# Sliding attention and a GeGLU block on one core: ones of the crossed units in their own tile, clears and spreads of both pairs in one GpSimd instruction, another order of the staged v, and other PSUM banks for one unit's scores

## The chip, the core and the metric

The kernel runs on one core of a Trainium2 chip. The metric is the device time of one execution in microseconds, as the median of several runs. Names used below: PE is TensorE, DVE is VectorE, ACT is ScalarE, POOL is GpSimd and SP is SyncE, which only issues DMAs here. A "q" behind an engine's name means its sequencer, which waits and issues.

## The reference

The inputs are q, k and v of 8 batches, 8 heads, 576 tokens and 64 dimensions each, and three weight matrices. Heads 0 to 3 attend to the last 32 tokens ("plain"), heads 4 to 7 to every fourth of the last 128 ("dilated"). The heads' outputs, put side by side, are the 4608 x 512 input of a gated feed-forward block.

```python
scores = scale * np.matmul(q, k.transpose(0, 1, 3, 2))
rel = pos[:, None] - pos[None, :]
mask_plain = (rel >= 0) & (rel < 32)
mask_dil = (rel >= 0) & (rel < 128) & (rel % 4 == 0)
attn = softmax(np.where(masks, scores, -1e9))       # heads 0-3 plain, 4-7 dilated
x = np.matmul(attn, v)                              # to 4608 x 512
g, val = x @ w_gate, x @ w_val                      # 512 -> 1536
out = (0.5 * g * (1 + erf(g / sqrt(2))) * val) @ w_out
```

## The kernel before

**Units.** The attention of one batch is cut into four units of two heads each; the two heads of a unit lie on the two halves of the 128 partitions. Unit n belongs to batch n // 4. In batches 0, 1 and from 4 on, the first two units of a batch are plain and the last two dilated; in batches 2 and 3 it is the other way round (`pair`, `is_plain`). A batch's two plain units share tiles for q, k and v, and so do its two dilated ones; the index g (0 or 1) says which of the two units is meant and x which half of the partitions.

**Steps of a unit.** A program in words gives the order in which each engine gets its work. `S4@2` is the scores of unit 4 in PSUM bank 2 and the one after it, `P4` the exp on ACT, `M4` the multiplication with a mask on DVE, `D4` the sums (a matmul with ones), `T4` and `B4` or `A4` the reciprocal of the sums, `N4` the matmul with v, `X4` the product of both into `xT`. `t8` to `t15` are the transposes of q and k of batch 1 by matmul (`turn_first`). A digit alone is so many matmuls of the feed-forward block. `g` and `u` are the gelu on ACT and the product on DVE that makes `u_all`; `e0` to `e3` are the copies of 128 output rows to one of four `osb` buffers, each followed by a store that SP issues. `E` and `G` load ACT's tables. `V`, `V1`, `F2` and `H2` are `second()`, `second_v()`, `load_first(2)` and `load_rest(2)`, which issue loads and the work of POOL for the coming batches.

**Block-diagonal tiles.** For batches from 1 on, the scores and `N` are matmuls over all 128 partitions. A block of k or v is 128 x 128 with the two heads in two of its four 64 x 64 quarters and zeros in the others. In the second unit (g = 1) the heads stand crossed: the head of half x goes to column half 1 - x. `zero()` clears the unused quarters, with one memset per g and x; `spread()` copies k into the used quarters from `dense`; `cast_v()` does this for v out of `stage`. The sums of crossed units need crossed ones, so `two_ones` has two 128 x 128 parts: part 0 is set by DVE at the start, part 1 by two POOL memsets in `second()`.

**Feed-forward.** The 4608 rows go through in nine chunks of 512. A chunk has 96 matmuls for gate and value (L635) and 48 for the output (L642). The units of a batch stand between those of the chunk that comes before its rows. In chunk 0 the last gate (block 11) is in bank 2 and its value in bank 3.

**Queues around the change.** POOL runs in the order written: `second()` comes after batch 0's units and issues, behind its clears, the loads of batch 1's q and k (`six`, then `load_eights`, both with a cast to f16), the last weights and `wo` in three pieces. SP runs in its order too: the v loads of batch 1 (`load_v(1, ...)`) wait for the second `wo` piece to land, then come `load_first(2)`, two stores, `load_rest(2)` with four DMA transposes (L267) and eight small and large loads of dilated v (L244, L248), a store, `load_first(3)` and then the store of `e3` of chunk 0 with those of chunk 1.

**Lines that the prediction uses.** L107 and L116 are POOL's first instructions (`identity`, `bands`), L132 the end of the masks, L152 and L155 the weight loads, L175 `load_eights`, L200 the memset in `zero`, L215 and L227 the casts of q and k, L256 the cast in `cast_v`, L275 the copy in `spread`, L323 the tail of dilated q, L364 and L360 the copies in `turn_first` on DVE and ACT, L382 its transposes, L441 the matmuls of units, L503 the exp, L653 the copies `e`, L657 the stores, L728 the memsets of `two_ones` in `second()`, L804 the product `u`.

## Time and profile before

| | |
|---|---|
| median of 6 runs | 342.13 us (341.26 to 343.46) |
| the profiled execution's own time | 341.77 us |
| its span (first to last instruction) | 340.1 us |
| granted clock of PE | 1.00 |
| PE busy | 327.3 us |
| DVE, ACT, POOL busy | 157.5, 157.7, 153.9 us |
| moved by DMA | 47.96 MB, mean 141 GB/s |

The profile is one execution. Its first part gives busy times of the engines, its fourth the chain of work that ended last. Beside the page the trace can be asked who waited for whom, for a timeline of an engine in a stretch of time (start, length, engine, line, operation, tiles, shapes, count, and in brackets the idle time before and what ended it), and for the busy shares in given stretches. Times in timelines count from the start of the span. A line of a timeline can hold several instructions of a kind; its length then reaches over all of them.

### The profile page before, as it was taken

How to read it: one execution, taken by the hardware profiler on the slowest of the kernel's cores; microseconds unless marked ns; L12 is line 12 of the kernel's file. 1: busy time of each engine (PE TensorE's matmuls, PEld its weight loads, DVE VectorE, ACT ScalarE, POOL GpSimd, SP SyncE). 2: the span in 40 equal slices, each digit the busy share in tenths (PEclk: the TensorE clock that was granted, in tenths of full speed). 3: DMA queues.
4: the chain of work that ended last, by engine and by line, in shares of the span. 5: the costliest groups of instructions: out<-in, count | busy, mean ns of one | idle time of the engine just before them, and what ended most of it. 6: DMA issues, size and time to landing. Idle time of an engine off the chain costs nothing.

```text
span 340.1 us, 7089 instructions
## 1 busy us (share of the span) xinstructions
PE 327.3 (96%) x2780; PEld 164.0 (48%) x2780; DVE 157.5 (46%) x245; ACT 157.7 (46%) x235; POOL 153.9 (45%) x291
## 2 busy tenths in 40 slices
PE   7899899998979999999999999999999999999995
PEld 5654454443534455445554454445544444444443
DVE  6764454443624445432585365367854424303310
ACT  2663466534653358436943573345534343223321
POOL 8799877759335746835944762682000000000000
PEclk9999999999999999999999999999999999999999
DMA  8999995897689589769889947982100110020002
GB/s 188 185 181 151 201 187 139 207 213 173 153 275 201 139 224 197 201 168 215 154 230 214 188 152 180 249 149 83 64 0 3 63 62 2 0 93 33 0 31 95
DMA packets 109250, 47.96 MB, mean 141 GB/s; under 512 B 83872, under 2 KB 104736, under 8 KB 109216
## 3 DMA queue, kind: packets, MB, share of 16 engines
q1 hardware_dynamic: 97440, 39.99, 50.8%
q0 software_dynamic: 11216, 6.79, 14.1%
q10 hardware_dynamic: 560, 0.72, 0.8%
q8 instruction: 22, 0.36, 0.4%
q14 instruction: 12, 0.10, 0.1%
HBM read 37.75 MB, written 9.44 MB: 139 GB/s over the span
## 4 chain that ended last, share of the span: by engine, by line
PE 76%; DMA 9%; POOL 7%; SPq 4%; issue 1%; ACT 1%; DVE 1%; POOLq 0%; DVEq 0%; ACTq 0%
PE ps L635 44%; PE ps L642 24%; PE ps L441 4%; PE ps L452 3%; DMA xT<-in_q_dram 2%; DMA xT<-in_k_dram 2%; DMA out_dram<-osb 2%; SPq L208 1%; DMA dense<-s 1%; DMA stage<-in_k_dram 1%; POOL wv L152 1%; POOL wg L152 1%; POOL v L256 1%; POOL q L200 1%; PE ps L666 1%
## 5 line engine op out<-in xcount | busy, mean ns | idle before, releaser
L804 DVE SCALAR_TENSOR_TENSOR u_all<-g,ps 128x512 f16<-128x512 f16 x108 | 73.8, 687 | 111.7 <-PE ps L635 100.3
L635 PE MATMUL ps<-xT,wv 128*128 128x512 f16 x432 | 112.8, 379 | 2.2 <-ACT osb L653 2.2
L635 PE MATMUL ps<-xT,wg 128*128 128x512 f16 x432 | 114.2, 379 | 0.4 <-ACT g L799 0.2
L799 ACT ACTIVATE g<-ps 128x512 f16<-128x512 f32 x108 | 64.0, 597 | 108.2 <-PE ps L635 108.0
L642 PE MATMUL ps<-wo,u_all 128*128 128x512 f16 x420 | 99.0, 379 | 0.0
L635 PEld LDWEIGHTS <-wv 128*128 128x128 f16 x432 | 42.2, 98 | 50.6 <-issue 0.3
L635 PEld LDWEIGHTS <-wg 128*128 128x128 f16 x432 | 41.6, 98 | 51.8 <-issue 3.7
L642 PEld LDWEIGHTS <-u_all 128*128 128x128 f16 x420 | 38.0, 98 | 39.9
L275 POOL COPY q<-dense 64x512 f16<-64x512 f16 (+1 forms) x84 | 40.5, 519 | 20.3 <-DMA dense<-s 12.5
L256 POOL CAST v<-stage 64x576 f16<-64x576 f32 x60 | 41.0, 684 | 7.3 <-DMA stage<-in_v_dram 4.4
L503 ACT ACTIVATE P<-ps 128x832 f16<-128x832 f32 (+1 forms) x32 | 26.7, 834 | 21.3 <-PE ps L441 15.6
L626 DVE TENSOR_TENSOR xT<-ps,rb 128x576 f16<-128x576 f32 x32 | 29.8, 935 | 14.5 <-PE ps L452 9.8
L653 ACT ACTIVATE osb<-ps 128x512 f32<-128x512 f32 x34 | 20.2, 593 | 28.8 <-PE ps L642 23.6
L215 POOL CAST s<-stage 128x640 f16<-128x640 f32 x24 | 16.6, 718 | 33.6 <-DMA stage<-in_q_dram 21.3
L227 POOL CAST s<-stage 128x512 f16<-128x512 f32 x24 | 14.4, 631 | 11.2 <-DMA stage<-in_q_dram 6.7
L508 DVE TENSOR_TENSOR P<-P,two_d 128x768 f16<-128x768 f16 x14 | 9.1, 649 | 16.4 <-ACT P L503 16.4
L441 PE MATMUL ps<-q 128*128 128x96 f16 (+2 forms) x225 | 13.4, 203 | 1.7 <-POOL q L323 0.9
L605 ACT ACTIVATE lg<-ps 128x576 f32<-128x576 f32 x17 | 11.1, 650 | 7.5 <-PE ps L452 6.5
L441 PEld LDWEIGHTS <-q 128*128 128x128 f16 x225 | 11.3, 98 | 5.8 <-issue 1.9
L508 DVE TENSOR_TENSOR P<-P,two_p 128x832 f16<-128x832 f16 x14 | 8.6, 616 | 10.6 <-ACT P L503 9.0
L452 PEld LDWEIGHTS <-v 64*64 64x64 f16 x400 | 9.2, 107 | 8.6 <-issue 7.3
L596 DVE STREAM_TRANSPOSE dt<-ps 128x576 f32<-128x576 f32 x15 | 11.6, 775 | 2.5 <-ACT rb L607 1.7
(76 smaller groups left out, 197.9 us busy)
## 6 DMA issues: line engine op xcount, KB each, us to landing
out_dram<-osb SPq DMA_DIRECT2D x35, 256.0 KB, 2.3
stage<-in_v_dram SPq DMA_DIRECT2D x32, 144.0 KB, 3.8
stage<-in_v_dram SPq DMA_DIRECT2D x28, 128.0 KB, 2.7
stage<-in_q_dram SPq DMA_DIRECT2D x24, 128.0 KB, 3.0
stage<-in_k_dram SPq DMA_DIRECT2D x24, 128.0 KB, 2.8
stage<-in_q_dram SPq DMA_DIRECT2D x6, 512.0 KB, 4.4
stage<-in_k_dram SPq DMA_DIRECT2D x6, 512.0 KB, 5.5
wg<-in_moe_w_gate_dram POOLq DMA_DIRECT2D x6, 256.0 KB, 6.6
```

Source lines behind the costliest of these rows:

```text
L256: nc.gpsimd.tensor_copy(dst[half, at, half_of(x, g * swap)], st[half, at])
L275: eng.tensor_copy(dst[half, :, :, half_of(x, g)], src[half])
L441: nc.tensor.matmul(o, lhs, rhs, start=st, stop=end, skip_group_check=True)
L452: nc.tensor.matmul(o[cols], lhs[rows, cols], rhs[rows], start=st, stop=end, skip_group_check=True)
L503: nc.scalar.activation(pt[:, 0 : src.shape[1]], src, AF.Exp, bias=0.0, scale=scale)
L508: nc.vector.tensor_tensor(pt, pt, mask, ALU.mult)
L626: nc.vector.tensor_tensor(dst, num, rb, ALU.mult)
L635: nc.tensor.matmul(ps[:, bank, :], w[:, kc, ns], xT[kc][:, tok], start=first, stop=end)
L642: nc.tensor.matmul(ps[:, bank, :], u_all[:, fc, tb * P : (tb + 1) * P], wo_t[fc // 4][:, fc % 4, :], start=(fc == 0), stop=(fc == NNB - 1),)
L653: nc.scalar.activation(osb, ps[:, bank, :], AF.Copy, bias=0.0, scale=1.0 / USCALE)
L799: nc.scalar.activation(g, ps[:, gate_banks(c, args[0])[0], :], AF.Gelu)
L804: nc.vector.scalar_tensor_tensor(u_all[:, nb, :], tiles.pop(("g", nb)), USCALE, val, ALU.mult, ALU.mult)
```

## The change

Five edits stand in it.

1. `two_ones` keeps only the straight ones. The crossed ones get a tile of their own, `ones_two`, cleared and set by three POOL memsets in `second_v()`, between the clears of batch 2's k and the casts of batch 1's v. The two memsets of `second()` go.
2. `zero()` gives one memset for each half x, over the blocks of both g, where it gave one for each g and x.
3. `spread_plain()` gives one copy for each x over both g, where it gave two; in `spread_dil()` the small copy of the last block is given once for each x, behind the two large ones.
4. `load_v()` stages dilated v by the place of the head (x) and not by g, and issues the four large loads first and then the four small ones, where a small one followed each large one; `cast_v()` reads accordingly.
5. The scores of unit 4 go to banks 4 and 5, where they went to 2 and 3.

```diff
-    two_ones = const.tile([P, 2, P], F16, tag="two_ones")
+    two_ones = const.tile([P, P], F16, tag="two_ones")
+    ones_two = const.tile([P, P], F16, tag="ones_two")
...
     def zero(t, eng=nc.gpsimd, gs=(0, 1), swap=1):
-        for g in gs:
-            for x in range(2):
-                y = x ^ (g * swap)
-                part = t[64 * x : 64 * x + 64, NB2 * g : NB2 * g + NB2].bitcast(F32)
-                eng.memset(part[:, :, 32 - 32 * y : 64 - 32 * y], 0.0)
+        for x in range(2):
+            g = gs[0]
+            part = t[64 * x : 64 * x + 64].bitcast(F32)
+            first = 32 - 32 * (x ^ (g * swap))
+            step = NB2 * 64 + swap * (32 if x else -32) * (1 - 2 * g)
+            eng.memset(at2(part[:, NB2 * g], first, [[step, len(gs)], [64, NB2], [1, 32]]), 0.0)
...
         for g in range(2 - 2 * plain):
             for x in range(2):
-                half = st[half_of(x, g), 576 * g : 576 * g + 576]
-                rows_ = v[b, HK + 2 * g + x]
-                nc.sync.dma_start(
-                    out=half[:, 0:512].rearrange("p (i c) -> p i c", i=2),
-                    in_=rows_[0 : 4 * P].rearrange("(i p r) d -> p i (r d)", i=2, r=4),
-                )
-                nc.sync.dma_start(out=half[:, 512:576], in_=rows_[S - 64 : S])
+                half = st[half_of(x, g), 576 * x : 576 * x + 512]
+                rows_ = v[b, HK + 2 * g + x, 0 : 4 * P].rearrange("(i p r) d -> p i (r d)", i=2, r=4)
+                nc.sync.dma_start(out=half.rearrange("p (i c) -> p i c", i=2), in_=rows_)
+        for g in range(2 - 2 * plain):
+            for x in range(2):
+                at = slice(576 * x + 512, 576 * x + 576)
+                nc.sync.dma_start(out=st[half_of(x, g), at], in_=v[b, HK + 2 * g + x, S - 64 : S])
...
-    def cast_v(dst, i, gs=(0, 1), swap=1):
+    def cast_v(dst, i, gs=(0, 1), swap=1, plain=1):
...
             for x in range(2):
-                half = half_of(x)
-                nc.gpsimd.tensor_copy(dst[half, at, half_of(x, g * swap)], st[half, at])
+                y = x ^ (g * swap)
+                src = g if plain else y
+                at, of = (slice(NB2 * i, NB2 * i + NB2) for i in (g, src))
+                nc.gpsimd.tensor_copy(dst[half_of(x), at, half_of(y)], st[half_of(x), of])
...
+    def spread_two(dst, src, x):
+        half, step = half_of(x), NB2 * P + (-64 if x else 64)
+        n = src.shape[2] // 64
+        base = dst[half, 0, 64 * x : 64 * x + 1]
+        out_ = bass.AP(tensor=base.tensor, offset=base.offset, ap=[base.ap[0], [step, 2], [P, n], [1, 64]])
+        nc.gpsimd.tensor_copy(out_, src[half].rearrange("p g (j c) -> p g j c", c=64))
...
     def spread_plain(kp):
         for x in range(2):
-            for g in range(2):
-                src = kdp[:, g : g + 1, 0:S].rearrange("p g (j c) -> p g j c", c=64)
-                spread(nc.gpsimd, kp[:, NB2 * g : NB2 * g + NB2].rearrange("p (g j) c -> p g j c", g=1), src, x, g)
+            spread_two(kp, kdp[:, :, 0:S], x)
...
-                last = NB2 * g + 8
-                spread(
...
+            spread_two(kd[:, 8:], rest, x)
...
-        ones_of = two_ones[:, odd(n), :]
+        ones_of = ones_two if odd(n) else two_ones
...
     def second():
         load_w(4)
-        for x in range(2):
-            nc.gpsimd.memset(two_ones[half_of(x), 1, half_of(x, 1)], 1.0)
         for t in views(1)[2:]:
             zero(t)
...
     def second_v():
         for t in views(2)[2:4]:
             zero(t)
+        nc.gpsimd.memset(ones_two, 0.0)
+        for x in range(2):
+            nc.gpsimd.memset(ones_two[half_of(x), half_of(x, 1)], 1.0)
         cast_v(views(1)[4], 1)
-        cast_v(views(1)[5], 2)
+        cast_v(views(1)[5], 2, plain=0)
...
-            "V1 F2 S4@2 E P4 11 M4 S5@2 1 P5 3 D4@0 M5 ...
+            "V1 F2 S4@4 E P4 11 M4 S5@2 1 P5 3 D4@0 M5 ...
```

## The prediction, made before the change ran

> **What bounds the kernel now.** I read the page first (busy shares and the chain), then the waits of PE, then the chain in order of time, then the timelines of GpSimd, SyncE and PE around each wait, and last the single records (issue, landing, semaphore) behind them.

> ```profile
> PE 327.3 (96%) x2780; PEld 164.0 (48%) x2780; DVE 157.5 (46%) x245; ACT 157.7 (46%) x235; POOL 153.9 (45%) x291
> PE 76%; DMA 9%; POOL 7%; SPq 4%; issue 1%; ACT 1%; DVE 1%; POOLq 0%; DVEq 0%; ACTq 0%
> ```

> TensorE is busy for 96% of the span and no matmul changes, so the change can only touch the idle stretches. The waits of PE name them (total us, times, longest):

> ```profile
> PE ps L635 <- ACT osb L653: 2.2, 1, 2.2
> ...
> PE ps L382 <- DMA xT<-in_q_dram: 1.1, 1, 1.1
> ...
> PE ps L441 <- POOL q L323: 0.9, 1, 0.9
> PE ps L441 <- DVE u_all L804: 0.6, 1, 0.6
> ...
> PE ps L441 <- POOL q L275: 0.2, 1, 0.2
> ```

> PE's timeline puts them in place: t12 waits at 39.39, S4 at 44.82, S8 at 81.53 and 82.79, and a matmul of chunk 1 or 2 waits for the store copy e3@1 at 99.94. After 102 us no single wait of PE is over 0.3 us, so what is gained by 102 us stays gained. GpSimd's timeline ahead of t12, and SyncE's two ends of a long run of issues:

> ```profile
> 22.05 0.33 POOL L728 MEMSET two_ones<- 64x64 f16 x2
> 22.41 2.92 POOL L200 MEMSET q<- 64x288 f32 x8
> 25.36 2.92 POOL L200 MEMSET v<- 64x288 f32 x8
> 28.23 0.69 POOL L732 DMA_DIRECT2D s<-in_q_dram  x1
> ```
> ```profile
> 46.13 2.64 SPq L239 DMA_DIRECT2D stage<-in_v_dram  x4
> ...
> 92.47 7.78 SPq L657 DMA_DIRECT2D out_dram<-osb  x5
> ```

> The chain runs through those clears, through `31.05 8.29 DMA xT<-in_q_dram` (the eights of batch 1) to t12, and later through SyncE's issues to `92.47 6.74 DMA out_dram<-osb` (the store e3@0), which holds the fourth buffer that e3@1 needs.

> **second(), ahead of t12.** Sixteen clears start 0.37 us apart. No row shows a clear of both pairs. Slope: `L107` (128 elements a lane) takes 0.204 us and `L728` (64) 0.146, 0.91 ns per element, so 288 more elements cost 0.26 and a merged clear 0.63 against 0.74 for two: 0.11 saved, eight times 0.88. Bounds: no saving at all, or all of the 64-element row and its 0.04 gap as fixed price, 0.19 each, 1.5. A loss through a deeper pattern I leave to a rival: the three-level `L227` copy of 512 takes 0.61 like the 512 of `L275`. I take 0.88, since the rows are of the same operation. The two memsets of `two_ones`, 0.37 from 22.04 to 22.41, leave too. The loads of batch 1 are thus issued 1.25 earlier (0.37 to 1.85). Landing is bounded by the queue ahead: load_w(4) lands last at 29.68, and six DMAs of 256 KB land 1.27 apart. The 288 KB of q took until 32.58; at that pace they would land at 31.1, at the 1.94 that the next 288 KB took at 31.6. So everything behind (q, k, weights, eights, wo) moves by s = 0.96 to 1.47, or 0.37 if merging saves nothing; I take s = 1.1. t12 gets back min(1.11, s) = 1.1.

> At the very start DVE clears half as much (`two_ones`, 0.165; the 64-element memsets 0.11): 0.05 at most ahead of GpSimd's band. The first eights' landing at 12.26 may follow. Taken as 0.

> **S4 in banks 4 and 5.** It waited 0.59 for u11, the DVE product of banks 2 and 3. Banks 4 and 5 were last read by ScalarE's copies of t13, over at 43.11; with t12 earlier that is 42.0, and S4 stands at 42.75. So 0.59 is gone. What is late next: P4 follows the table load, which ended 0.07 before it, so P4 moves by 1.1 and not 1.7; M4 ended 1.85 before D4, of which 1.26 is left. wo: the ninth output matmul needs the second wo piece (landed 46.12, used 46.70), the seventeenth the third (48.99, used 49.51). PE would come 1.69 earlier and wo 1.1, so margins of 0.58 and 0.52 become 0 and -0.07: PE's gain here is at most s + 0.5 = 1.6.

> **second_v().** Clears of kp and kd: 8 to 4, 0.44 saved. `ones_two` costs 0.20 + 2 x 0.146 + 0.12 of gaps = 0.61 on GpSimd; behind it the casts of v wait 0.61 for a DMA anyway, and the spreads before it got shorter, so nothing. Without that cover it would be 0.61 against N5, which has 55.74 - 54.73 = 1.0. The fourteen later clears become seven: 0.77 saved, from 57.76 on. Behind them stands the cast of q, and SyncE waits from 63.56 to 64.36 for it with the load of dilated k: up to 0.8 for SyncE's line.

> **Dilated v staged by place.** The same eight DMAs, 0.645 apart on SyncE, the four small ones last. The first dilated cast now waits for the fifth, not the second; the fifth landed at 54.81 and that cast started at 54.79. In batch 2 the fifth landed at 82.43, the cast started at 82.69. So 0 to 0.1 on GpSimd, hidden by N6's 1.5; without that cover, 0.1 on PE. The queue behind (casts, then loads of the next batch) keeps its last landing, the eighth.

> **Spreads.** 576 elements take 0.665, 512 take 0.612: 0.83 ns each and 0.19 fixed, 0.06 of that overlapped. Plain: two instructions fewer, 0.26 per batch; dilated: two small ones of 0.18 fewer, 0.05 more in each left, 0.25 per batch. S8 waits behind both (0.23 and 0.92).
> Beside longer copies: the cast at 84.14 took 0.94 instead of 0.66 next to a mask multiply (84.00 to 84.56), so the two engines do hold each other up. [...] By the trace no multiply stands beside a spread (spreads 73.76 to 76.35 and 79.30 to 82.39, multiply at 84.00), so I count 0.

> **Where the end is set.** The v loads of batch 1 wait for the second wo piece at 46.12, and from there SyncE issues nearly without a break to 92.47. So its line moves by S = s plus some of the 0.8; I take 0.3 of it, because the loads and stores around it (landing at 67.17, 69.92, 70.56, 71.29) share the DMA. S = 1.4, between 0.4 and 2.3. At S8 GpSimd is S + 0.5 = 1.9 earlier and PE 1.6, so 0.3 of its 1.15 goes and PE is 1.9 earlier. At e3@1 PE must wait for the store, which is only S earlier: the wait grows from 2.2 to 2.7, and the gain from there on is S = 1.4.

> Sum: the profiled execution took 341.77 (span 340.1 and 1.67 around it), to become 340.4; it lies 0.36 under the median of 342.13, so the forecast is 342.13 - 1.4 = 340.7.

> **Rivals.** (1) *Given back at e3@1.* Matmuls gain at t12, S4 and S8, but the store e3@0 lands where it did, because DMA and not issue paces 54 to 99 us. For: 6.7 us from issue to landing. Against: by the stretches of the trace the DMA share is 0.64 from 54 to 64, 1.10 to 72, 1.14 to 78 and 0.66 to 92, under the 1.40 of the weights from 16 to 28, and the transfers of that stretch begin with the v loads, which move. Gain 0 to 0.6, time 341.8.
> (2) *Merging saves nothing.* A clear costs by its elements and gap. Then s = 0.37, S = 0.4, time 341.7. For: the gap of 0.04 is all that the rows show between clears. Against: the 0.09 that the slope leaves at zero elements.
> (3) *Slower: the merged clear costs more per element.* Place: second(), eight of them before the loads. It decides from (5.92 + 0.37) / 8 = 0.79 us a piece on. At 0.95 (1.6 ns per element) the loads go 1.3 later, t12 waits 2.4, wo and SyncE follow, and the end with them: 343.4. Against: every GpSimd row of this size lies near 1 ns per element.

> **How the numbers follow.** Forecast 0.64, (1) 0.18, (2) 0.08, (3) 0.10. Its own range is 339.8 (S = 2.3) to 341.1; a bound of 0.3% (1.03 us) is about what a measurement can tell here. (1) and (2) lie within it but for the best end of (1), 0.01. So faster 0.65, same 0.25, slower 0.10. The range reaches to (1) and (2) with 0.2 of spread, 342.3, and leaves out (3).

> **What would show it.** Right: clears of 64x576 with 0.6 to 0.65 from start to start; `s<-in_q_dram` issued near 27.0; no wait of t12 over 0.2 and none of S4; the v loads on SyncE near 45.0; S8's waits near 0.9 together; a wait of 2.5 to 2.8 at e3@1; a span of 338.7. Wrong: clears of 0.74 or more, the second wo piece still at 46.1, or e3@0 still landing at 99.2.

## The result

| | before | after |
|---|---|---|
| median | 342.49 us (69 runs, 340.56 to 346.41 and one of 567.72) | 341.28 us (32 runs, 339.02 to 342.79) |
| ratio | | 0.9958, 95% interval 0.9945 to 0.9972 |
| the profiled execution, its span | 341.77, 340.1 us | 341.86, 340.2 us |
| granted clock of PE in it | 1.00 | 0.993 |

The change is faster by 1.2 us, 0.42%; 340.7 was forecast, in a range of 339.8 to 342.3. The profiled execution of after is no faster than that of before, though, and this is what had to be explained. The page of after, its busy times, its row of granted clocks and its chain:

```profile
PE 328.1 (96%) x2780; PEld 164.1 (48%) x2780; DVE 158.6 (47%) x243; ACT 157.7 (46%) x235; POOL 148.5 (44%) x246
...
PEclk9999999999989999999999999999999999999999
...
PE 77%; DMA 13%; POOL 7%; SPq 1%; issue 1%; ACT 0%; DVE 0%; POOLq 0%; ACTq 0%
```

GpSimd works 5.4 us less with 45 instructions fewer. PE has as many matmuls as before and is busy 0.8 us longer, and one slice of the clock's row, about 94 to 102 us, is an 8: some matmuls ran slower. GpSimd's timeline (start, length, engine, line, what, count) and SyncE's, at the places that were shown of before:

```profile
21.85 2.40 POOL L206 MEMSET q<- 64x576 f32 x4
24.29 2.40 POOL L206 MEMSET v<- 64x576 f32 x4
26.64 0.69 POOL L733 DMA_DIRECT2D s<-in_q_dram  x1
```
```profile
45.28 2.64 SPq L245 DMA_DIRECT2D stage<-in_v_dram  x4
...
91.45 7.64 SPq L660 DMA_DIRECT2D out_dram<-osb  x5
```

A merged clear goes every 0.61 us (from 21.85 to 24.29, four of them), the loads of batch 1 are issued 1.59 earlier, the v loads 0.85 and the store e3@0 1.02. PE's waits, and its timeline where it waited between 36 and 106 us:

```profile
PE ps L638 <- ACT osb L656: 2.8, 1, 2.8
...
PE ps L448 <- POOL q L330: 0.7, 1, 0.7
PE ps L645 <- DMA wo<-in_moe_w_out_dram: 0.7, 1, 0.7
```
```profile
45.31 0.81 PE L645 MATMUL ps<-wo,u_all 128*128 128x512 f16 x3 [0.66 <-DMA wo<-in_moe_w_out_dram]
81.02 0.33 PE L448 MATMUL ps<-q 128*128 128x80 f16 x5 [0.70 <-POOL q L330]
98.78 0.38 PE L638 MATMUL ps<-xT,wv 128*128 128x512 f16 x1 [2.82 <-ACT osb L656]
```

The waits of t12 and S4 are gone, as forecast. The matmuls of S4 that had waited start 2.22 us earlier than before, those behind the wo pieces 1.15, those of S8 1.77, and the matmul behind e3@1 1.16 (98.78 against 99.94). Then the windows (length, busy time of each engine, granted clock, DMA share) show this, of after and of before:

```profile
100.00:104.00 4.00, 4.00 (x13) 1.32 (x10) 1.28 (x2) 1.72 (x4) 0.00 (x0) 0.57 1.03 203
```
```profile
100.00:104.00 4.00, 3.76 (x17) 1.58 (x17) 1.45 (x3) 2.87 (x4) 0.00 (x0) 1.00 0.89 195
```

In the 4 us behind the long wait the clock of after is 0.57; in the records it is one stretch at 0.5 that begins at 100.08, 1.3 us after PE took up work again, and lasts 3.41. Its matmuls stand 0.43 apart and not 0.216. So the 1.16 gained at 98.78, and 0.24 of a wait for a gelu that went too, are spent by 103.6, where PE stands 0.2 behind the kernel before: the half clock cost it 1.6. At the end PE is 0.1 behind.

That is one execution. Each run gives its mean clock: in 10 of 33 of after (the 32 and one more) it was 0.998 or more, and their median is 340.08; in the other 23 it lay from 0.990 to 0.995, with 341.57. The kernel before loses clock as well, though its profile shows none: 342.11 in 25 runs at full clock, 343.06 in the 40 others (its runs beside the experiments, without three that were over 1.5% slower than its fastest). So by these medians after is 2.0 faster where neither loses clock, and a loss of clock costs it 1.5 where it costs before 0.95.

### The profile page after: what moved, and what is told of

Its sections match the earlier page's. It is cut to its first block, busy times and chain, and to the rows that moved or that the text cites. A ratio compares the mean times of both kernels' runs of the same rounds, so it can differ in the third digit from the quotient of the medians.

```text
span 340.2 us, 7043 instructions
## 1 busy us (share of the span) xinstructions
PE 328.1 (96%) x2780; PEld 164.1 (48%) x2780; DVE 158.6 (47%) x243; ACT 157.7 (46%) x235; POOL 148.5 (44%) x246
## 4 chain that ended last, share of the span: by engine, by line
PE 77%; DMA 13%; POOL 7%; SPq 1%; issue 1%; ACT 0%; DVE 0%; POOLq 0%; ACTq 0%
PE ps L638 44%; PE ps L645 25%; DMA wo<-in_moe_w_out_dram 5%; PE ps L448 4%; DMA stage<-in_v_dram 3%; PE ps L459 3%; DMA out_dram<-osb 2%; DMA u_all<-in_q_dram 2%; DMA stage<-in_k_dram 2%; SPq L245 1%; POOL wv L153 1%; POOL wg L153 1%; PE ps L669 1%; POOL v L206 1%; POOL q L283 1%; POOL q L206 1%
## 5 line engine op out<-in xcount | busy, mean ns | idle before, releaser
L291 POOL COPY q<-dense 64x1152 f16<-64x1152 f16 (+1 forms) x28 | 20.6, 734 | 15.8 <-DMA dense<-s 13.8
L283 POOL COPY q<-dense 64x512 f16<-64x512 f16 x28 | 17.3, 645 | 3.9 <-ACT dense L367 1.6
L515 DVE TENSOR_TENSOR P<-P,two_d 128x768 f16<-128x768 f16 x14 | 9.4, 670 | 16.0 <-ACT P L510 16.0
L515 DVE TENSOR_TENSOR P<-P,two_p 128x832 f16<-128x832 f16 x14 | 9.6, 689 | 10.6 <-ACT P L510 10.4
```

What stands on the lines that cost most here:

```text
L283: eng.tensor_copy(dst[half, :, :, half_of(x, g)], src[half])
L291: nc.gpsimd.tensor_copy(out_, src[half].rearrange("p g (j c) -> p g j c", c=64))
```

## The experiments

Three questions stood behind them: which edit carries the gain, whether the idle stretch at e3@1 brings the clock down, and where the gain goes that S4, the spreads and S8 show and the end does not. The theory at the start: the clears move GpSimd's DMA queue, that moves the wo pieces, SyncE's line and the store e3@0, and S4's banks only move a wait; what is gained ahead of e3@1 beyond that is lost in its wait and in the clock behind it. The rivals are with each run.

**S4's banks alone**, in the kernel before.

```diff
-            "V1 F2 S4@2 E P4 11 M4 S5@2 ...
+            "V1 F2 S4@4 E P4 11 M4 S5@2 ...
```

> Only the edit of S4's banks, on the kernel before. Theory (the end is set by when the store e3@0 lands, which follows SyncE's line of issues from the second wo piece on): S4's wait of 0.59 is gone, PE comes 0.5 earlier to the output matmuls, but GpSimd's and SyncE's lines stand still, so S8 waits 0.5 longer (1.6 in all), e3@1 waits 2.2 as before, and the time is the same within 0.3 us. Rival (each removed wait of PE counts by itself): 0.6 us faster than before, S8's wait as before.

Measured: 342.86 us in 12 runs, ratio 0.9995 (0.9964 to 1.0027). PE's timeline of it:

```profile
45.93 0.81 PE L642 MATMUL ps<-wo,u_all 128*128 128x512 f16 x3 [0.43 <-DMA wo<-in_moe_w_out_dram]
82.28 0.34 PE L441 MATMUL ps<-q 128*128 128x96 f16 x4 [1.50 <-POOL q L275]
83.55 0.45 PE L441 MATMUL ps<-q 128*128 128x80 f16 x5 [0.92 <-POOL q L323]
```

S4's 0.59 is gone and comes back as 0.43 at the second wo piece and as a longer wait at S8 (2.42 together, where before has 1.15 and the theory 1.6): the banks alone buy nothing that 12 runs can tell (the interval is 1.1 us to either side). Right behind S8's two waits, at 83.62, the clock is at 0.5 for 3.41 us here too, at another place and with another releaser. PE comes to e3@1 2.4 later than in the kernel before, so e3@1 waits only 0.19 and not the 2.2 of the theory. The windows of it show the half clock as 0.58 over 4 us:

```profile
83.00:87.00 4.00, 3.45 (x13) 1.46 (x13) 0.56 (x1) 1.22 (x2) 3.44 (x6) 0.58 0.74 197
```

**The clears and the ones alone** (edits 1 and 2) in the kernel before: `zero()`, `two_ones` and `ones_two` as in the changed kernel, spreads, v and S4 as before.

> Only the merged clears and the crossed ones in their own late tile, on the kernel before. Theory: second() ends about 1.6 us earlier, the second wo piece lands 0.8 to 1.3 us earlier, SyncE's line and e3@0 follow, t12's 1.11 is gone and S4's 0.59 stays; S8's waits about 1.1; the end is 1.0 to 1.3 us earlier before any clock change, nearly all of the full change's gain. Rival (each wait counts by itself): 1.1 us faster and e3@0 lands where it did (99.2).

Measured: 341.30 us in 12 runs, 0.9958 (0.9927 to 0.9989), the whole change's ratio. The second wo piece landed at 44.20 in its profile (46.12 before, 45.27 after), the store e3@0 was issued at 90.45, and PE waited 2.01 for e3@1 until 97.91, 2.03 earlier than before. The piece moved by 1.92, more than the 0.8 to 1.3 of the theory. With four buffers these two edits give the whole gain, as far as 12 runs can tell it (1.1 us to either side).

**The change without S4's banks** (`S4@2` again).

> The full change but for S4's banks, which stay 2 and 3. Theory: S4 waits 0.6 again, the waits for wo at the output matmuls (0.74) shrink by as much, e3@0 lands as in the full change, and the time is that of the full change within 0.3 us. Rival (each wait counts by itself): 0.6 us slower than the full change.

Measured: 341.15 us in 12 runs, 0.9958 (0.9930 to 0.9986). S4 waits 0.59 again, e3@1 only 1.90 and the matmul behind it starts at 97.43. The store e3@0 landed at 96.70, 1.35 earlier than in the profile of after, where the theory had it unmoved. The median shows no loss: together with the run of the banks alone, no worth of the fifth edit is seen with four buffers, and one well over 1 us would have been.

**Work in the wait.** Ten matmuls of ones, whose result is not used, stand ahead of the matmul that waits for e3@1 in the changed kernel. They use the idle time and take 2.32 us.

```diff
-4 N11@1 e3@1 R 1 X11 G 7 g0 3 g1 u0
+4 N11@1 e3@1 R 1 X11 G 4 W10@4@0 3 g0 3 g1 u0
```

> The full change plus ten idle matmuls of 512 columns (2.2 us, into bank 4, result unused) put ahead of the matmul that waits for e3@1. Theory (the long idle stretch there makes the granted clock fall to 0.5 for 3.4 us in about two runs of three, which costs 1.5 us each time): the clock is 1.00 over the span in nearly all runs, the idle stretch is 0.6 us, and the median falls by about 1.0 us below the full change, to 2.2 to 2.6 us below before. Rival (the clock falls for another cause): mean clocks of 0.993 as often as without them, time the same or up to 0.3 us slower than the full change.

Measured: 340.94 us in 12 runs, 0.9967 (0.9947 to 0.9987). 11 of 12 runs were at 0.998 or more of the clock, where the changed kernel had 10 of 33. PE's timeline around the wait, and much later:

```profile
95.43 2.32 PE L692 MATMUL ps<-ones 128*128 128x512 f16 x10
98.18 0.38 PE L638 MATMUL ps<-xT,wv 128*128 128x512 f16 x1 [0.43 <-ACT osb L656]
...
171.09 0.81 PE L638 MATMUL ps<-xT,wv 128*128 128x512 f16 x3 [1.24 <-ACT osb L656]
```

The idle stretch brings the clock down in this kernel: nothing else was changed, and with useless work in it 1 of 12 runs lost clock, where 23 of 33 had. But the time did not follow: by the medians it fell by 0.3 of the 1.0 that I expected, by the ratios to before (0.9967 against 0.9958) not at all, and these full-clock runs (340.96) are slower than the changed kernel's (340.08). The third line shows a new wait, of 1.24 us, 70 us on: the chain of waits there leads through `167.15 3.21 DMA out_dram<-osb`, the store e3@2, which SyncE issued behind eight v loads, to the copy e3@3, which needs its buffer. The prediction's statement that nothing after 102 us takes time back was wrong: e3@3 does it when the store e3@2 lands late. It landed at 170.36 here and at 172.21 with S4's banks alone, where PE, though later than before, waited 0.91 for e3@3 (at 172.94). With the clears and ones alone and without S4's banks PE came there over 2 us earlier than before and waited under 0.3, as that store landed at 168.40 and 167.68 (170.87 before).

**Five buffers.** That gives the wait its cure: a fifth `osb` buffer, 2 KB more of each partition (512 elements of 4 bytes). In the changed kernel and in the kernel before:

```diff
-    osbp = ctx.enter_context(tc.tile_pool(name="osbp", bufs=4))
+    osbp = ctx.enter_context(tc.tile_pool(name="osbp", bufs=5))
```

> The full change with five buffers for the output copies instead of four, so that e3@1 waits for the store e2@0 (issued at 80.9) and not for e3@0. Theory: the wait of 2.82 at e3@1 and the fall of the clock after it are gone; PE keeps its 1.8 us of S8 and gains the 2.2 of e3@1 and 0.2 of the gelu behind it: 4.0 to 4.3 us faster than before, 2.5 to 3 faster than the full change. Rival (the loads and casts behind set the end as well): another wait of 1 us or more in the next 20 us, gain under 2.5 us.

> The kernel before with five buffers for the output copies. Theory: the wait of 2.21 at e3@1 and the 0.24 behind it are gone, 2.2 to 2.5 us faster than before (more if before too loses clock in some runs); the full change with five buffers is 1.6 to 1.9 us faster than this one, since PE's gain up to S8 is then kept. Rival: as for the full change, a new wait behind takes over, gain under 1.5 us.

Measured: 336.44 us (336.01 to 336.74, 6 runs) for the changed kernel, ratio to before 0.9818 (0.9785 to 0.9851); 339.20 us (338.56 to 341.08, 6 runs) for the kernel before with five, 0.9903 (0.9868 to 0.9938). The first beats both kernels of this case, by 4.8 and 6.0 us; both gains are larger than expected (4.0 to 4.3 and 2.2 to 2.5 against the kernel before). PE's waits of the first, whole but for the start's `ones`, and of the second, with their totals, numbers and longest:

```profile
PE ps L389 <- DMA xT<-in_k_dram: 0.9, 1, 0.9
PE ps L448 <- POOL q L330: 0.5, 1, 0.5
PE ps L448 <- POOL v L264: 0.3, 1, 0.3
PE ps L495 <- DVE dense L371: 0.2, 1, 0.2
PE ps L386 <- DVE s L371: 0.2, 1, 0.2
```
```profile
PE ps L382 <- DMA xT<-in_k_dram: 1.1, 2, 0.9
PE ps L441 <- POOL q L323: 0.9, 1, 0.9
PE ps L379 <- DVE s L364: 0.7, 1, 0.7
PE ps L382 <- DMA xT<-in_q_dram: 0.6, 1, 0.6
PE ps L441 <- DVE u_all L804: 0.6, 1, 0.6
PE ps L488 <- DVE dense L364: 0.3, 1, 0.3
PE ps L441 <- POOL v L256: 0.3, 1, 0.3
PE ps L441 <- POOL q L275: 0.2, 1, 0.2
```

No line names `osb` any more, in either. All six runs of the first are at full clock. By its sum of waits, 2.1 against 4.7, the change should give 2.6 here; by the medians it gives 2.76. So with four buffers less than half of what the change buys ahead of 100 us reached the end (1.2), and with five nearly all: the rest was held back at e3@1 and e3@3 and by the clock. The buffer also took more than the wait and the clock account for: 4.8 us off the changed kernel, where the wait of 2.82 and the clock (1.5 in 23 of 33 runs, 1.0 on average) make 3.9, and 3.3 off the kernel before (342.49 to 339.20), where the wait of 2.21 and the clock (0.95 in 40 of 65 runs, 0.6) make 2.8. Part of the rest may be waits like that of e3@3, which the profiled executions with four buffers did not all have; it is not shown.

**Undoing one edit at a time, with four buffers**: v staged as before, and the spreads as before.

> The full change but dilated v staged and issued as before. Theory: nothing on PE's path, SyncE's line the same length; the same time as the full change within 0.3 us, e3@0 landing within 0.3 of 98.05. Rival (the order of the small loads matters): more than 0.5 us of difference at e3@0.

> The full change but k spread with one copy for each unit as before. Theory: GpSimd's line to S8 is 0.5 us longer, so S8 waits 0.5 more (1.2); the wait at e3@1 is 0.5 shorter (2.3), which keeps the time ahead of the clock, but makes the fall of the clock rarer: same as the full change, or up to 0.7 us faster. Rival (shorter GpSimd work counts at the end): 0.5 us slower than the full change.

Measured, 12 runs each: 340.53 us with the old v, 0.9949 (0.9918 to 0.9979); 341.92 us with the old spreads, 0.9977 (0.9949 to 1.0005). The first cannot be told from the change (0.9958), at full clock (340.09) or without (341.74). Its store e3@0 landed at 96.58, though, and not within 0.3 of 98.05: the rival's difference of over 0.5 is there, but without a worth, and as this landing lies between 96.58 and 98.56 in the profiles with merged clears and four buffers, one profile cannot put it down to the order of v. The second looks 0.6 slower, though its interval holds 0.9958 too; parted by clock it is 0.4 slower in both groups (340.45 in 3 runs, 341.99 in 9). The theory's shorter wait (2.3) and rarer falls of the clock did not come: 9 of 12 runs lost clock, and the profile shows the worst of it, a wait of 3.14 for e3@1 and two half-clock stretches in one, 6.83 us from 98.43 on:

```profile
99.29 0.59 PE L647 MATMUL ps<-xT,wv 128*128 128x512 f16 x1 [3.14 <-ACT osb L665]
```

With four buffers the runs of each of these two kernels are spread over 4.5 and 3.9 us, the clock's 1.5 among it, which hides terms of half a microsecond.

**Undoing one edit at a time, with five buffers.** No store stops PE here, all of these runs have full clock, and the runs of each kernel but the last lie within 1.6 us of each other. Four kernels, each the changed one with five buffers and one edit taken back: S4's banks, the spreads, `zero()`, the order of dilated v.

> The changed kernel with five osb buffers, but the scores of unit 4 in banks 2 and 3 as before. With five buffers no store stops TensorE, so what an edit is worth at S8 stays to the end; the bases are 336.44 us for the changed kernel with five buffers and 339.20 for the kernel before with five. Theory (the banks only move a wait): S4 waits 0.59 again and S8's wait of 0.51 for GpSimd shrinks by as much, so the time is within 0.2 of the changed kernel with five buffers, 336.3 to 336.7. Rival (the banks are worth their wait once nothing behind takes it back): 0.6 slower, 337.0, with S8's wait still near 0.5.

> The changed kernel with five osb buffers, but the spreads as before. Theory (S8 waits for GpSimd, which the four extra copies make 0.35 to 0.5 later): S8's waits grow from 0.5 to 0.9 or 1.0 together and the time by 0.35 to 0.5, to 336.8 or 336.9. Rival (with four buffers the 0.65 by which the old spreads looked slower came from the clock alone): S8's waits grow, but less than 0.15 of it is left at the end.

> The changed kernel with five osb buffers, but zero() as before (16 memsets of 64x288 ahead of the loads of batch 1 where 8 of 64x576 stand, 28 in all where 14 stand). Theory (the merged clears carry most of the gain, through GpSimd's DMA queue): 8 x (0.74 - 0.61) = 1.04 more ahead of the loads; t12 waits 0.3 to 0.7 again, the second wo piece lands 0.5 to 0.7 later and GpSimd stands that much and 0.4 more later at S8, so the time is 0.6 to 1.2 longer, 337.0 to 337.6. Rival (taking the two memsets of ones out of second() and the shorter spreads carry it): 0.4 longer at most, 336.8.

> The changed kernel with five osb buffers, but dilated v staged, loaded and cast in the order of before. Theory (the order of the staged v is worth nothing): within 0.2 of the changed kernel with five buffers, and if anything 0.1 to 0.2 faster, since GpSimd's dilated casts no longer wait for the fifth load and S8 waits for GpSimd. Rival (the order of the loads carries part of the gain): over 0.3 slower, 336.8 or more, and S8's wait longer than 0.5.

Measured (the base ran on another chip; the kernel before took 342.36 beside it and 342.33 beside these four), with the delay of PE in the one profiled execution of each against that of the base. The delay is taken at the same 512-column matmul: the 240th behind the first (76.61 us in the base, ahead of S8), the 280th (88.27, behind it) and the 600th (168.62).

| taken back | median us (runs) | against 336.44 | profiled run | delay ahead of S8 | behind S8 | at 168 us |
|---|---|---|---|---|---|---|
| S4's banks | 337.17 (6, 336.10 to 337.68) | +0.73 | 337.17 | 0.27 | 1.26 | 1.15 |
| spreads | 336.77 (5, 336.56 to 337.42) | +0.33 | 336.72 | 0.64 | 0.82 | 0.71 |
| clears | 337.91 (5, 337.73 to 338.62) | +1.47 | 338.62 | 1.26 | 2.62 | 2.50 |
| v's order | 336.95 (6, 335.82 to 339.01) | +0.51 | 339.01 | 0.44 | 1.43 | 3.01 |
| all five (before, five buffers) | 339.20 (6) | +2.76 | 338.56 | 1.87 | 2.66 | 2.54 |

Two things in these delays are hardly the edits'. The executions differ from the start: at the 20th such matmul, ahead of GpSimd's clears, PE stands at -0.50, -0.09, 0.05, -0.18 and 0.11 against the base, in the table's order. And the base's profiled run is the fastest of its six, those of the clears and of v's order the slowest of theirs, so their delays lie above what the medians show.

*Clears.* The main term, and larger than the 0.6 to 1.2 of the theory; the rival's 0.4 is out. GpSimd's clears of it, then PE's three waits that come back or grow, in two views:

```profile
21.90 2.92 POOL L205 MEMSET q<- 64x288 f32 x8
24.86 2.92 POOL L205 MEMSET v<- 64x288 f32 x8
```
```profile
38.79 0.71 PE L388 MATMUL ps<-ident,xT 72*64 72x72 f16 x32 [0.67 <-DMA xT<-in_q_dram]
45.74 0.81 PE L644 MATMUL ps<-wo,u_all 128*128 128x512 f16 x3 [0.27 <-DMA wo<-in_moe_w_out_dram]
81.31 0.34 PE L447 MATMUL ps<-q 128*128 128x96 f16 x4 [0.90 <-POOL q L282]
```

It issues the loads at 27.72 (1.08 later than the base's 26.64), its second wo piece lands at 45.70 (base 44.49) and its v loads start at 45.71 (44.51). The path is the one that the prediction followed.

*Spreads.* 0.33, just under the 0.35 to 0.5 of the theory. S8's wait is 0.69 and not 0.9 to 1.0: in the profiled execution only 0.18 of the delay arises at S8, and 0.64 stood already ahead of it, at a wo piece that landed later (44.98 against 44.49) behind the same instructions. Of the clock there is nothing in it, which speaks against the rival (under 0.15), and the 0.4 by clock groups with four buffers agrees; but 0.33 is less than two executions of the same stretch differ.

*S4's banks.* The theory's 0.2 is missed, and the rival's 0.6 nearly met, but not in the rival's manner: S8's waits are 0.54 and 0.80, where it has 0.51 to stay. PE is 0.27 late ahead of S8 though it started 0.50 early, since 0.79 is lost at S4; 0.99 more comes at S8, since GpSimd's cast of dilated q waited 2.41 for its load (0.99 in the base). What the banks do to that load, if anything, the profile does not say.

*v's order.* By its median over the rival's 0.3, and S8's waits, 0.52 and 0.80, are longer as the rival has it; but with four buffers the old order was not slower, and this kernel has both the fastest (335.82) and the slowest run of the four. Its profiled one is the slowest, with a wait that no other profile with five buffers has:

```profile
162.31 0.54 PE L446 MATMUL ps<-q 128*128 128x96 f16 x9 [1.63 <-POOL q L289]
```

The chain leads to it through loads of q and the transpose `154.60 4.98 DMA dense<-s`, so GpSimd was late here by landings too. The worth of the two small edits, the banks and v's order, stays open at 0 to 0.7 us each: landings in the crowded stretch from 44 to 80 us differ between the profiled executions (the second wo piece came 0.49 later with the old spreads behind the same instructions, and the cast of dilated q waited 1.42 longer for its load with S4's banks taken back).

## Why the prediction was right, point by point

| step | forecast | measured in after |
|---|---|---|
| merged clear, start to start | 0.63 | 0.61 |
| loads of batch 1 issued earlier | 1.25 | 1.59 |
| PE's gain at the start, by 32 us | 0 | 0.24 |
| eights of q and k landed earlier | 1.1 | 1.47, 1.23 |
| wo pieces landed earlier | 1.1 | 0.86, 0.85, 0.68 |
| PE's gain behind wo | 1.6 at most | 1.15 |
| PE's gain at S8 | 1.9 | 1.77 |
| S, the store e3@0 earlier | 1.4 | 1.02 issued, 1.16 landed |
| wait at e3@1 | 2.7 | 2.82 |
| span | 338.7 | 340.2 |

**Clears, right.** The price came from the slope of two other memset rows and lay 0.02 over the measured one. Rival 2 (nothing saved, 0.74) and rival 3 (0.95) are out. The issue moved by 0.34 more than counted, as 0.2 of it stood already ahead of the first clear (21.85 against 22.05). That, and PE's 0.24 at the start, need not be the change's: in the profiles with merged clears, the same program up to there, the first clear starts anywhere from 21.44 to 21.95.

**The queue behind, direction right, size off.** I let one s of 1.1 hold for everything on GpSimd's queue. In the profile the shift shrinks along it, from 1.59 at the issue to 0.85 at the second wo piece, and other executions of kernels with merged clears had that piece at 44.15 to 44.98, 1.1 to 2.0 earlier than before. So one s was a fair middle, not a constant.

**S4, right in the trace and without a worth that the four-buffer runs could show.** The wait went, and wo's margins (forecast 0 and -0.07) became waits of 0.66 and 0.08. That the cap of s + 0.5 takes the bank change back was in the prediction, and both four-buffer runs on it agree, within the 1.1 us that they can tell.

**S8 and the spreads, right.** 1.77 against 1.9, one wait of 0.70 against 0.9. The price of longer copies was put at 0 from one batch, and in another a mask multiply does meet a merged copy: `129.68 1.57 DVE L515 TENSOR_TENSOR P<-P,two_p`, where the one at 126.57 takes 0.59, beside a copy of k from 129.67 to 130.81. That is 0.98 more. No wait of PE over 0.3 follows it, so at the end the 0 held.

**v's staging, hidden as said.** The cast at 53.76 waited 0.91 for the fifth load, which landed at 53.71, more than the 0 to 0.1 counted, and PE did not wait for it.

**e3@1, right; what follows it, wrong.** The wait grew as worked out and took the rest of the gain. Rival 1 (the store lands where it did) is out: it landed 1.16 earlier. The step that failed is the sentence that no wait of over 0.3 stands after 102 us and so what is gained by then stays gained. It priced an idle stretch at its own length. The longer stretch cost PE another 1.5 us by half clock in two runs of three. And where the store e3@2 lands late, e3@3 waits (0.91 in the run of S4's banks, 1.24 with work in the wait).

**The number, in part luck.** Where neither kernel loses clock the change is worth 2.0 and not the 1.4 of S, so S was too small (the store e3@0 landed 1.16 earlier in the profile of after, and 0.65 to 2.63 earlier in the other profiles with merged clears and four buffers); and the clock, which the sum leaves out, takes back more of it in after (1.5 in 23 of 33 runs) than in before (0.95 in 40 of 65). The two misses have opposite signs, and 340.7 lies between the runs with full clock (340.08) and without (341.57). The range held because its upper end was drawn for a gain given back by another mechanism.

## To carry to other kernels

When a change lets PE run ahead of a buffer that a store holds, the gain can become idle time there (2.82 us here, where it was 2.21); look first for what frees the buffer, since one more of 2 KB a partition was worth four times this change. To judge small edits, first take such a stop out: here it hid their worth in its wait and, with the clock's 1.5 us, scattered the runs of the two kernels tried so over 4.5 and 3.9 us, where with five buffers those of each changed kernel but one lay within 1.6. And a merged instruction paid most here where DMA issues stand behind it on the same engine: the merged clears, 1.1 us ahead of the loads, were worth 1.47 us at the end with five buffers.

## What the hardware showed that was not expected

The stretches at one clock that begin ahead of PE's last matmul are whole numbers of 3.41 us long in the profiles of after and before: in after, 95.57 us at full clock from 4.51 on (28 of them), 3.41 at half clock and 235.52 at full clock (69); in before, 334.51 at full clock from 6.95 on (98). Cut into windows of 3.41 us from the start of its first stretch, after has the first of these lines and before the next two, into which its wait of 2.21 falls; the last, around its wait of 1.90, is of the change without S4's banks (length, busy time of PE and of the other engines, granted clock, DMA):

```profile
96.67:100.08 3.41, 1.30 (x7) 0.58 (x7) 0.00 (x0) 1.92 (x3) 1.74 (x4) 1.00 0.53 198
95.70:99.11 3.41, 2.03 (x18) 1.04 (x17) 0.83 (x2) 0.68 (x1) 1.67 (x3) 1.00 1.02 371
99.11:102.52 3.41, 2.34 (x11) 0.99 (x11) 0.69 (x2) 2.97 (x4) 0.68 (x2) 1.00 0.67 185
94.14:97.56 3.42, 1.52 (x15) 0.74 (x12) 0.76 (x1) 0.82 (x3) 2.34 (x4) 1.00 1.00 377
```

Behind the first the clock was 0.50 for 3.41 us, behind the next two 1.00, and the profiled run of the last has a mean clock of 0.999. In the 3.41 us ahead of the other two falls PE worked 1.13 us (from 95.02, old spreads) and 0.99 (from 80.20, S4's banks alone). So PE was idle for 2.11, 2.28 and 2.42 us of the 3.41 ahead of the three falls, and for 1.90, 1.38 and 1.07 in the windows shown that kept the clock. With the old spreads PE worked 2.55 of the first 3.41 us at half clock, and 3.41 more at half clock followed; in after it worked all of the 3.41, and full clock came back. That the idle time of such a window is what decides is not shown: there are three falls ahead of PE's end, and these windows leave 1.90 to 2.11 open. Nor is it shown why a kernel loses clock in some of its runs only, after in 23 of 33 and before in 40 of 65.
